# A decode block on one core: the last block of the modulation weight, split into uneven pieces on SyncE's and GpSimd's queues

## The chip, the cores and the metric

The kernel runs on one core of one Trainium2 chip. The metric is the device time in microseconds: 1050.39 us is the median of three runs of the kernel before (1050.29 to 1050.45).

## What is computed

One token passes through a transformer block with adaptive layer norms. The reference, cut to what matters (all in float32):

```python
mod = (_silu(c) @ w_mod).reshape(1, 6, 1, 640)      # sa, ca, ga, sb, cb, gb
h = _layernorm(x) * (1 + ca) + sa
x = x + ga * attention(h, k_cache, v_cache, wq, wo)  # 32 heads, 8192 positions, 192 wide
h = _layernorm(x) * (1 + cb) + sb
x = x + gb * (relu(h @ w1 + b1) ** 2 @ w2 + b2)      # 640 -> 1536 -> 640
```

`w_mod` is 640 x 3840. K and V cache are 32 x 8192 x 192 each, and they make nearly all of the 452 MB that the kernel reads.

## The kernel before, in words

**One stream of loads.** Every large input is laid out on the host as rows of 128 partitions and read once, in order, by transfers issued by SyncE's queue (`nc.sync.dma_start`, SP in the profile): `wm0` (L131), six pieces of `wm0x` (L134), then 53 chunks of the cache and of `wq` and `wo` (`load`, L236 to L253; the last chunk in two transfers), then `wm1`, `w1` and `w2` in several cuts each. They go into three slots of 16128 columns a partition, `slots` (L563), in turn: `wm0_t` in the first, chunk 0 in the second, chunk 1 in the third, chunk 2 again in the first. `load(n + 3)` is called after the work on chunk n (L436), so chunk 2 waits until the slot of `wm0_t` has been read for the last time, chunk 3 until chunk 0 has been worked off, and so on.

**The start.** `wm0` holds the first 1280 columns of `w_mod` (shift and scale of the first norm) as five blocks of 128 rows, the first block of `wq`, and small vectors. `mod(0, 2, wm0_t, wm0x_t)` (L193, called at L257) multiplies silu(c) with these columns on TensorE: four groups of 32 output partitions, each with its quarter of the 640 columns of both vectors, `DG` = 160 columns each. Blocks 0 to 3 are whole. Of the last block, `wm0` holds five of the eight quarters; the other three, `WX` = 480 columns, are held apart in `wm0x`: each of the block's 128 rows has one piece of 480 columns (1920 bytes). The table `XP` (L42) places the pieces: an entry (a, k, n) is one transfer of k rows to the partitions a, a+4, ..., with the first n of `SX` = 7 places a row. A place that no piece fills stays zero from the two memsets at L129 and L130, and the coefficients `cx` put silu(c) of the right row at each place and partition, so that 7 small matrix products with 64 partitions for each of two output groups (L211 to L214) add up what the block's missing quarters give. Then come the first norm, `query(0, ...)` (L273), which turns the first block of `wq` into the query of the first heads, and from there the loop over the chunks (L389).

**The loop.** For each chunk VectorE multiplies K with the query (`multiply`, L285) and sums over the 192 columns (`scores`, L293), GpSimd adds halves of 7/16 of the rows (L411), and TensorE applies V (`values`, L334) and `wo` (`attend`, L366 and L368).

**The end.** `w2` comes in six transfers, and in `finish` (L476) the matrix products of each wait for that transfer alone. After the last, two small operations of VectorE and the two transfers of the result follow.

**Partitions and DMA engines.** A transfer to 128 partitions is split over the core's 16 DMA engines in equal shares, 8 rows an engine. A transfer of fewer rows uses fewer engines: the trace has the eight rows of the first piece transfer on eight engines at once, those of three rows on three.

Of the kernel before, what the change touches and what calls it, by code (L numbers as in the profile page):

```python
# [13 lines left out]
P = 128  # L14
D = 640
# [4 lines left out]
G = 4  # L20
DG = D // G
FG = FF // G
KB = DG // 32
# [14 lines left out]
UNIT = E * DH  # L38
EXTRA = {"o": WO, "q": WQ}
SLOT = 84 * DH  # L40
SX = 7
XP = ((32, 8, 5), (0, 3, SX), (1, 3, SX), (2, 3, SX), (3, 3, 6), (33, 1, SX))  # L42
WX = 3 * DG
W0 = KB * 2 * D - WX
VPC = 5
LEAD_FROM = 1300
# [51 lines left out]


@with_exitstack  # L100
def block_kernel(ctx: ExitStack, tc: tile.TileContext, kept, kv, wm0, wm0x, wm1, w1, w2):
    nc = tc.nc
    const = ctx.enter_context(tc.tile_pool(name="const", bufs=1))
    work = ctx.enter_context(tc.tile_pool(name="work", bufs=2))
# [5 lines left out]
    def slot(name):  # L110
        taken.append(name)
        return kept["slots"][(len(taken) - 1) % 3]
# [12 lines left out]
    nc.gpsimd.memset(eps_t, EPS)  # L125

    wm0_t = slot("wm0_t")
    wm0x_t = wm0_t[:64, SLOT - SX * WX:]
    nc.vector.memset(wm0x_t[:, :SX // 2 * WX], 0.0)  # L129
    nc.gpsimd.memset(wm0x_t[:, SX // 2 * WX:], 0.0)  # L130
    nc.sync.dma_start(wm0_t[:, :wm0.shape[1]], wm0)  # L131
    r = 0
    for a, k, n in XP:
        nc.sync.dma_start(wm0x_t[a:a + 4 * k:4, :n * WX], wm0x[r:r + k, :n * WX])  # L134
        r += k

    small = const.tile([P, 2 * KB + SX + FB + KB], F32, name="small")
    nc.vector.tensor_copy(small, wm0_t[:, W0 + WQ:wm0.shape[1]])
    x_c, c_c, bbc = small[:, :KB], small[:, KB:2 * KB + SX], small[:, 2 * KB + SX:]

# [44 lines left out]
    e = const.tile([P, KB + SX], F32, name="silu")  # L185
# [7 lines left out]
    def mod(first, n, w, wx=None, between=lambda: None):  # L193

        ps = psum.tile([P, 512], F32, tag="q", name=f"ps_mod{first}", bufs=2)
        for b in range(KB):
            if b == 3:
                between()
            wb = w[:, b * n * D:(b + 1) * n * D]
            if wx is None or b < KB - 1:  # L200
                wb = wb.rearrange("p (m n) -> p m n", m=n)
                parts = [(g, slice(0, n * DG), wb[:, :, DG * g:DG * (g + 1)]) for g in range(G)]
            else:
                wb = wb[:, :n * 3 * DG].rearrange("p (m n) -> p m n", m=n)
                parts = [(g, slice(0, n * DG), wb[:, :, DG * g:DG * (g + 1)]) for g in range(2)] + [(2, slice(0, DG), wb[:, 0, 2 * DG:])]
            for g, at, wg in parts:
                nc.tensor.matmul(ps[32 * g:32 * (g + 1), at], e[:, b:b + 1].to_broadcast([P, 32]), wg,  # L207
                                 start=(b == 0), stop=(b == KB - 1 and (wx is None or g < 2)))
        if wx is not None:
            wx = wx.rearrange("p (s n) -> p s n", s=SX)  # L210
            for s in range(SX):  # L211
                for g, at, wg in ((2, slice(DG, 2 * DG), wx[:, s, :DG]), (3, slice(0, 2 * DG), wx[:, s, DG:])):
                    nc.tensor.matmul(ps[32 * g:32 * (g + 1), at], e[:64, KB + s:KB + s + 1].to_broadcast([64, 32]), wg,  # L213
                                     start=False, stop=(s == SX - 1))  # L214
        nc.vector.tensor_copy(mods[:, first:first + n], ps[:, :n * DG].rearrange("p (m n) -> p m n", m=n))

    def gate(m, w, steps):

        ps = psum.tile([P, 512], F32, tag="q", name="ps_gate", bufs=2)
        b = 0  # L220
        for n in steps:
            for b in range(b, b + n):
                for k in range(2):
                    nc.tensor.matmul(ps[64 * k:64 * (k + 1), :2 * DG], e[:, b:b + 1].to_broadcast([P, 64]),
                                     w[:, b, 2 * DG * k:2 * DG * (k + 1)], start=(b == 0), stop=(b == KB - 1))
            b += 1
            yield
        for g in range(G):
            r = slice(32 * g, 32 * (g + 1))
            nc.scalar.activation(m[r], ps[r, DG * (g % 2):DG * (g % 2 + 1)], AF.Copy)  # L230
        yield
# [23 lines left out]
    load(0)  # L255
    load(1)
    mod(0, 2, wm0_t, wm0x_t)  # L257
    ma = columns(mods[:, 0:2].rearrange("p m n -> p (m n)"), 2 * DG, "ma")
    h1 = layernorm(x_c, 1, lambda: ma[:, KB:, 0], lambda: ma[:, :KB, 0], "ln1")
# [129 lines left out]
    for n, (kp, nk, vp, nv, extra) in enumerate(PLAN):  # L389
# [3 lines left out]
        at = nk * DH + nv * UNIT  # L393
# [13 lines left out]
        if nk:  # L407
            multiply(kt, kp, nk)
            m = nk - POOL * nk // 16
# [34 lines left out]
    turn(NPAIR - 1)  # L444
    attend(*wo_t)
    mod(2, 3, wm1_t[:, KB * D:KB * 4 * D], between=gather)
    x1 = kept["x1"]
    nc.vector.tensor_mul(x1, att_t[0][:, :DG], mods[:, 2])
    nc.vector.tensor_add(x1, x1, x_t)

    last = gate(kept["gb"], gb_t, (2, 1, 2))
# [120 lines left out]
```

## Time and profile before

| | before |
|---|---|
| median of three runs | 1050.39 us |
| the profiled execution's own time | 1050.09 us |
| its span, first to last instruction | 1048.7 us |
| busy: VectorE, TensorE, GpSimd, ScalarE | 827.2, 491.7, 190.4, 44.9 us |
| HBM read | 451.82 MB |
| granted TensorE clock, mean | 0.72 |

A page of the profile gives busy times of each engine, the span in 40 slices, the DMA queues, the chain of work that ended last, and groups of instructions. "SPq" is the queue of SyncE that issues transfers; its duration is that of issuing, not of the transfer. q1 is the queue row on which SyncE's transfers run; q8 and q14 bring the engines' own instructions. In the view by windows, the share of DMA is that of the 16 engines together, and a packet counts where it starts, so that short windows with long packets read roughly.

### The profile page before, as it was taken

The numbers are of one execution on the slowest core, as the hardware profiler recorded it, in microseconds if no ns is written. First come the engines' busy times: TensorE is split into PE (matmuls) and PEld (weight loads), VectorE is DVE, ScalarE is ACT, GpSimd is POOL, SyncE is SP. The second block draws the span as 40 slices with busy tenths as digits, with TensorE's granted clock in tenths as the row PEclk, the third lists the DMA queues.
The fourth block names the chain that finished last, engine by engine and source line by source line (L and its number), as shares of the span: only waits on it lengthen the run. The fifth ranks groups of instructions, "written<-read, shape, count | busy, mean of one in ns | idle before, by whom it ended". The sixth has DMA issues, their size and how long they took to land.

```text
span 1048.7 us, 5220 instructions
## 1 busy us (share of the span) xinstructions
PE 491.7 (47%) x2162; PEld 136.0 (13%) x2162; DVE 827.2 (79%) x409; ACT 44.9 (4%) x122; POOL 190.4 (18%) x61
## 2 busy tenths in 40 slices
PE   3253334455352363436354366344445336436288
PEld 1010011111010010101011011011111002001023
DVE  1799878886959969888697895999887977988913
ACT  0100000000000000000000000000000000000001
POOL 1113121121212211212122121122221211311300
PEclk9676576777675686668766576676776767768689
DMA  9999999999999999999999999999999999999998
GB/s 408 431 434 433 432 433 433 440 437 439 436 437 431 431 433 432 433 433 429 435 439 436 436 432 432 434 431 433 433 434 431 436 448 434 433 433 431 423 425 365
DMA packets 9434, 452.16 MB, mean 431 GB/s; under 512 B 1066, under 2 KB 1326, under 8 KB 1710
## 3 DMA queue, kind: packets, MB, share of 16 engines
q1 hardware_dynamic: 9406, 451.83, 99.6%
q8 instruction: 17, 0.28, 0.1%
q14 instruction: 7, 0.05, 0.0%
q10 hardware_dynamic: 4, 0.00, 0.0%
HBM read 451.82 MB, written 0.00 MB: 431 GB/s over the span
## 4 chain that ended last, share of the span: by engine, by line
DMA 54%; DVE 33%; PE 12%; ACT 1%; issue 0%; SPq 0%; DVEq 0%; ACTq 0%
DMA slot<-in_kv 50%; DVE slot L285 17%; DVE sc L293 13%; PE ps_o L334 5%; DMA slot<-in_w 3%; PE ps_q L266 2%; PE att_a L366 2%; DMA slot<-in_wm 1%; DVE os L348 1%; PE ps_mx L309 1%; DVE om L346 1%; ACT p L317 0%; PE ps_mod L207 0%; PE att_a L368 0%; PE ps_mod L213 0%
## 5 line engine op out<-in xcount | busy, mean ns | idle before, releaser
L285 DVE TENSOR_TENSOR slot<-slot,qb 128x8064 f32<-128x8064 f32 (+19 forms) x81 | 419.7, 5212 | 127.0 <-DMA slot<-in_kv 121.8
L293 DVE TENSOR_REDUCE sc<-slot 128x25 f32<-128x4800 f32 (+21 forms) x109 | 333.9, 3096 | 0.4
L411 POOL TENSOR_TENSOR slot<-slot 128x1824 f32<-128x1824 f32 (+9 forms) x51 | 187.3, 3673 | 801.0 <-DVE slot L285 698.3
L334 PE MATMUL ps_o<-slot,p 128*32 128x512 f32 x1536 | 291.1, 724 | 70.4 <-DMA slot<-in_kv 60.8
L309 PE MATMUL ps_mx<-ident,mp 128*128 128x128 f32 x32 | 14.5, 452 | 346.4 <-DVE mp L307 346.4
L334 PEld LDWEIGHTS ps_o<-slot,p 128*32 128x32 f32 x1536 | 67.9, 130 | 268.7 <-issue 199.3
L366 PE MATMUL att_a<-slot,oW 128*32 128x512 f32 x96 | 66.5, 849 | 44.9 <-ACT oW L364 44.9
L266 PE MATMUL ps_q<-slot,ln_h 128*128 128x512 f32 x120 | 71.8, 758 | 27.2 <-DMA slot<-in_kv 25.0
L309 PEld LDWEIGHTS ps_mx<-ident,mp 128*128 128x128 f32 x32 | 5.6, 175 | 375.3 <-DVE mp L307 307.1
L317 ACT ACTIVATE p<-sc,nm 128x256 f32<-128x256 f32 x32 | 16.2, 507 | 650.3 <-DVE nm L311 650.3
L266 PEld LDWEIGHTS ps_q<-slot,ln_h 128*128 128x128 f32 x120 | 28.8, 250 | 67.4 <-issue 36.8
L346 DVE TENSOR_TENSOR om<-ps_o,mask 96x512 f32<-96x512 f32 x32 | 21.6, 675 | 8.9 <-PE ps_o L334 8.9
L311 DVE TENSOR_REDUCE nm<-ps_mx 128x1 f32<-128x128 f32 x32 | 9.3, 292 | 19.6 <-PE ps_mx L309 19.6
L366 PEld LDWEIGHTS att_a<-slot,oW 128*32 128x32 f32 x96 | 12.4, 144 | 82.3 <-ACT oW L364 47.6
L348 DVE TENSOR_REDUCE os<-om 96x64 f32<-96x512 f32 x32 | 21.8, 682 | 1.1
L356 DVE TENSOR_REDUCE oT<-ps_oT 128x3 f32<-128x96 f32 x16 | 4.0, 248 | 18.6 <-PE ps_oT L352 18.6
L322 PE MATMUL ps_sum<-ident,wide 128*128 128x128 f32 x16 | 7.5, 466 | 22.4 <-ACT wide L320 22.4
L352 PE MATMUL ps_oT<-ident,os 96*128 96x96 f32 x16 | 5.0, 314 | 25.3 <-DVE os L348 25.2
L207 PE MATMUL ps_mod<-slot,silu 128*32 128x480 f32 (+2 forms) x78 | 9.2, 612 | 14.3 <-DVE silu L189 14.3
L368 PE MATMUL att_a<-slot,oW 128*96 128x384 f32 x32 | 14.2, 525 | 0.0
L364 ACT ACTIVATE oW<-oT,r 128x96 f32<-128x96 f32 x16 | 5.9, 371 | 172.8 <-DVE oT L356 172.8
L267 ACT ACTIVATE qb<-ps_q 128x512 f32<-128x512 f32 x12 | 7.2, 597 | 131.9 <-PE ps_q L266 131.9
(84 smaller groups left out, 92.0 us busy)
## 6 DMA issues: line engine op xcount, KB each, us to landing
slot<-in_kv SPq DMA_DIRECT2D x38, 8064.0 KB, 35.3
slot<-in_kv SPq DMA_DIRECT2D x11, 8000.0 KB, 37.4
slot<-in_kv SPq DMA_DIRECT2D x2, 7872.0 KB
slot<-in_kv SPq DMA_DIRECT2D x1, 6144.0 KB, 22.7
slot<-in_wm SPq DMA_DIRECT2D x1, 4480.0 KB
slot<-in_wm SPq DMA_DIRECT2D x1, 4257.0 KB, 12.4
slot<-in_kv SPq DMA_DIRECT2D x1, 3264.0 KB
slot<-in_kv SPq DMA_DIRECT2D x1, 3072.0 KB
```

The lines of the kernel that those rows point to most:

```text
L266: nc.tensor.matmul(ps, h1[:, b:b + 1].to_broadcast([P, P]), w[:, b], start=(b == 0), stop=(b == KB - 1))
L285: nc.vector.tensor_mul(pr, pr, q[:, None, :].to_broadcast([P, b - a, DH]))
L293: nc.vector.tensor_reduce(sc[:, a % SRING:a % SRING + b - a], src[:, a - first:b - first], axis=AX.X, op=ALU.add)
L309: nc.tensor.transpose(ps[:, :P], mp.to_broadcast([P, P]), ident)
L311: nc.vector.tensor_reduce(nm, ps[:, :P], axis=AX.X, op=ALU.max, negate=True)
L317: nc.scalar.activation(p, s[:, :, None].to_broadcast([P, NPOS, 32 // E]), AF.Exp, bias=nm, accum_out=sp[:, h % 2:h % 2 + 1])
L334: nc.tensor.matmul(ps_t[h][32 * g:32 * (g + 1)], p[:, E * j:E * (j + 1)].rearrange("p e r -> p (e r)"), t[:, g], start=(j == 0), stop=last)
L346: nc.vector.tensor_mul(om[:n], ps_t.pop(h)[:n].rearrange("p (d e) -> p d e", e=E), mask[:n, None, :].to_broadcast([n, ED, E]))
L348: nc.vector.tensor_reduce(os_[:n, h % 2], om[:n], axis=AX.X, op=ALU.add)
L366: nc.tensor.matmul(att_a[96:, :512], oW[:, j], w[:, j, :512], start=(first and j == 0), stop=(last and j == NV - 1))
L368: nc.tensor.matmul(att_a[:96, :NV * (D - 512)], oW.rearrange("p j r -> p (j r)"), w[:, :, 512:], start=first, stop=last)
L411: nc.gpsimd.tensor_add(half, half, kt[:, m:, DH // 2:])
```

## The change

640 columns of the last block are taken out of `wm0` in place of 480: the third and fourth quarter of both vectors. `wm0` loses 160 columns of every partition. The 128 pieces are now 640 columns (2560 bytes) each, the places a row are `SX` = 12, and they may lie on all 128 partitions in place of 64.

57 pieces come in three transfers of SyncE: five rows with 3 places, three rows with 12, three rows with 2. The other 71 (and one place of zeros) come in three transfers of GpSimd's queue, two rows with 12 places each, to the partitions 28 and 64, 2 and 92, 29 and 65 (the table `XG`: rows of the transfer ahead, first partition, step). Ahead of each of these goes a tiny transfer of 7, 6 and 6 rows with two runs of 16 numbers a row, to columns that nobody reads. The rows of the new input `wm0y` are padded by 16 numbers after each place, which are not loaded, so a row of 12 places is 12 runs of 2560 bytes.

TensorE does two products of 320 columns over 128 partitions for each of the 12 places, and one product of 160 columns less in the last block. The two memsets cover 128 partitions and 12 x 640 columns in place of 64 and 7 x 480.

```diff
-SX = 7
-XP = ((32, 8, 5), (0, 3, SX), (1, 3, SX), (2, 3, SX), (3, 3, 6), (33, 1, SX))
-WX = 3 * DG
+SX = 12
+XP = ((32, 5, 3), (0, 3, SX), (1, 3, 2))
+XG = ((7, 28, 36), (6, 2, 90), (6, 29, 36))
+WX = 4 * DG
...
-    wm0x_t = wm0_t[:64, SLOT - SX * WX:]
+    wm0x_t = wm0_t[:, SLOT - SX * WX:]
     nc.vector.memset(wm0x_t[:, :SX // 2 * WX], 0.0)
     nc.gpsimd.memset(wm0x_t[:, SX // 2 * WX:], 0.0)
     nc.sync.dma_start(wm0_t[:, :wm0.shape[1]], wm0)
...
     for a, k, n in XP:
         nc.sync.dma_start(wm0x_t[a:a + 4 * k:4, :n * WX], wm0x[r:r + k, :n * WX])
         r += k
+    for i, (k, a, step) in enumerate(XG):
+        rest = wm0_t[32 * i:32 * i + k, wm0.shape[1]:wm0.shape[1] + 64].rearrange("p (a n) -> p a n", a=2)
+        nc.gpsimd.dma_start(rest[:, :, :16], wm0x[:k, :64].rearrange("p (a n) -> p a n", a=2)[:, :, :16])
+        to = wm0x_t[a:a + step + 1:step].rearrange("p (s n) -> p s n", n=WX)
+        nc.gpsimd.dma_start(to, wm0y[i, :, :, :WX])
...
-                wb = wb[:, :n * 3 * DG].rearrange("p (m n) -> p m n", m=n)
-                parts = [(g, slice(0, n * DG), wb[:, :, DG * g:DG * (g + 1)]) for g in range(2)] + [(2, slice(0, DG), wb[:, 0, 2 * DG:])]
+                wb = wb[:, :n * 2 * DG].rearrange("p (m n) -> p m n", m=n)
+                parts = [(g, slice(0, n * DG), wb[:, :, DG * g:DG * (g + 1)]) for g in range(2)]
...
             for s in range(SX):
-                for g, at, wg in ((2, slice(DG, 2 * DG), wx[:, s, :DG]), (3, slice(0, 2 * DG), wx[:, s, DG:])):
-                    nc.tensor.matmul(ps[32 * g:32 * (g + 1), at], e[:64, KB + s:KB + s + 1].to_broadcast([64, 32]), wg,
+                for g in (2, 3):
+                    wg = wx[:, s, 2 * DG * (g - 2):2 * DG * (g - 1)]
+                    nc.tensor.matmul(ps[32 * g:32 * (g + 1), :n * DG], e[:, KB + s:KB + s + 1].to_broadcast([P, 32]), wg,
                                      start=False, stop=(s == SX - 1))
...
+        "wm0y": np.pad(np.stack([xw[a:a + step + 1:step] for _, a, step in XG]), ((0, 0), (0, 0), (0, 0), (0, 16))),
```

More of the change, by code (lines that the diff above doesn't have):

```diff
@@ L100, in block_kernel @@
 @with_exitstack
-def block_kernel(ctx: ExitStack, tc: tile.TileContext, kept, kv, wm0, wm0x, wm1, w1, w2):
+def block_kernel(ctx: ExitStack, tc: tile.TileContext, kept, kv, wm0, wm0x, wm0y, wm1, w1, w2):
     nc = tc.nc
@@ L540 @@
     cc = column(c, KB)
-    at = [(s, a + 4 * i) for a, k, n in XP for s in range(n) for i in range(k)][:P]
+    at = [(s, a + 4 * i) for a, k, n in XP for s in range(n) for i in range(k)]
+    at = (at + [(s, a + i * step) for _, a, step in XG for s in range(SX) for i in range(2)])[:P]
     xs, xp = np.array(at).T
@@ L544 @@
     xw, cx = np.zeros((P, SX, WX), np.float32), np.zeros((P, SX), np.float32)
-    xw[xp, xs] = np.concatenate([last[:, 1, 2 * DG:3 * DG], last[:, 0, 3 * DG:], last[:, 1, 3 * DG:]], axis=1)
+    xw[xp, xs] = last.reshape(P, 2, G, DG)[:, :, 2:].transpose(0, 2, 1, 3).reshape(P, WX)
     cx[xp, xs] = cc[:, KB - 1]
@@ L549 @@
         "kv": np.concatenate(kv),
-        "wm0": np.concatenate([m0[:, :(KB - 1) * 2 * D], last[:, 0, :3 * DG], last[:, 1, :2 * DG],
+        "wm0": np.concatenate([m0[:, :(KB - 1) * 2 * D], last[:, 0, :2 * DG], last[:, 1, :2 * DG],
                                wq[0], column(A_x, KB), cc, cx, column(B_b1, FB), column(B_b2, KB)], axis=1),
         "wm0x": np.concatenate([xw[a:a + 4 * k:4] for a, k, _ in XP]).reshape(-1, SX * WX),
+        "wm0y": np.pad(np.stack([xw[a:a + step + 1:step] for _, a, step in XG]), ((0, 0), (0, 0), (0, 0), (0, 16))),
         "wm1": np.concatenate([rows(wm[:, 5 * D:], KB), rows(wm[:, 2 * D:5 * D], KB)], axis=1),
```

## The prediction

> **What bounds the kernel now.** I read the page's slices and queues first, then the end of the chain of waits, then the DMA share by windows around the end, then the start by timeline.
>
> ```profile
> DMA  9999999999999999999999999999999999999998
> q1 hardware_dynamic: 9406, 451.83, 99.6%
> q8 instruction: 17, 0.28, 0.1%
> HBM read 451.82 MB, written 0.00 MB: 431 GB/s over the span
> 1016.93 28.71 DMA slot<-in_w
> 1045.68 0.66 PE p_long L490 x16
> 1046.36 0.29 DVE slot L502
> ```
>
> All 16 DMA engines are busy in every slice: one stream of transfers is the kernel. 431 GB/s are 26.9 GB/s an engine. The chain ends with the last cuts of `w2` and 2.6 us of work behind them (1048.7 less about 1046.1), so whatever moves the last landing moves the end by as much. And the last landing is that of the slowest DMA engine, not of the mean:
>
> ```profile
> 1042.00:1043.00 1.00, 0.92 (x28) 0.95 (x32) 0.00 (x0) 0.00 (x0) 0.00 (x0) 1.00 1.00 406
> 1043.00:1043.50 0.50, 0.50 (x24) 0.50 (x20) 0.00 (x0) 0.00 (x0) 0.00 (x0) 1.00 0.92 367
> 1043.50:1044.00 0.50, 0.50 (x23) 0.50 (x17) 0.00 (x0) 0.00 (x0) 0.00 (x0) 1.00 0.81 325
> 1044.00:1045.00 1.00, 0.96 (x32) 0.50 (x21) 0.45 (x2) 0.00 (x0) 0.00 (x0) 1.00 0.77 315
> 1045.00:1045.50 0.50, 0.12 (x7) 0.00 (x0) 0.20 (x1) 0.00 (x0) 0.00 (x0) 1.00 0.74 284
> 1045.50:1045.80 0.30, 0.12 (x4) 0.12 (x8) 0.00 (x0) 0.00 (x0) 0.00 (x0) 1.00 0.75 258
> 1045.80:1046.00 0.20, 0.20 (x12) 0.20 (x13) 0.00 (x0) 0.00 (x0) 0.00 (x0) 1.00 0.36 109
> 1046.00:1046.20 0.20, 0.20 (x12) 0.04 (x4) 0.00 (x0) 0.00 (x0) 0.00 (x0) 1.00 0.08 22
> ```
>
> The last column but one is the DMA share. From 1043 to 1044 it falls to about 0.77 and stays there: four engines of 16 are through almost 3 us before the other twelve. Idle share times length adds up to 0.04 + 0.10 + 0.23 + 0.13 + 0.08 + 0.13 + 0.18 = 0.9 us. That is all that any better split over the engines can bring, since the bytes stay; 0.2% of the time, about what a measurement of this kernel can tell from no change, are 2.1 us.
>
> Why four are early is in the packet records, which the views only sum up. Each row starts 3 to 4 ns after the one before it on its engine, so the 16 chains can be followed. How far each is behind the earliest (1043.14) when its last row has landed, and why:
>
> ```
> 2.81 2.61 2.84                            engines 0-2: pieces of wm0x (39, 32, 32); the last two one 8 KB fetch each
> 2.99 2.95 | 2.69 | 0.79 | 0.01            engines 3-7: 5 pieces each; two 16 KB fetches | three of 8 KB | one | none
> 2.60 2.65 2.75 2.74 2.79 2.79 0.25 0.00   engines 8-15: no pieces; six with two 16 KB fetches each, two with none
> ```
>
> Which engine within a line is which the records don't tell. A fetch of instructions stops one engine's rows:
>
> ```profile
> q8 instruction: 1, 0.02, 4.8%
> q14 instruction: 1, 0.01, 1.0%
> ```
>
> These are windows of 1.2 us (from 62.4) and 2 us (from 119) with one fetch each: 4.8% of 16 engines over 1.2 us are 0.92 us, and 1.0% over 2 us 0.32. In the records the row behind it is late by another 0.3 to 0.5 us, 1.4 us in all for 16 KB. Sixteen such fetches before the end go round eight engines twice. The engines 0 to 2 have none, and so carry the pieces.
>
> **The change part by part.**
>
> ```profile
> slot<-in_kv SPq DMA_DIRECT2D x1, 8000.0 KB, 35.9
> slot<-in_kv SPq DMA_DIRECT2D x1, 6144.0 KB, 22.7
> slot<-in_wm SPq DMA_DIRECT2D x1, 4257.0 KB, 12.4
> slot<-in_kv SPq DMA_DIRECT2D x38, 8064.0 KB, 35.3
> 0.73 0.40 SPq L131 DMA_DIRECT2D slot<-in_wm  x1
> 1.42 1.69 POOL L130 MEMSET slot<- 64x1920 f32 x1
> 1.93 1.26 DVE L129 MEMSET slot<- 64x1440 f32 x1 [0.24 <-issue]
> 3.28 4.12 SPq L134 DMA_DIRECT2D slot<-in_wm0x  x6
> 7.45 27.21 SPq L249 DMA_DIRECT2D slot<-in_kv  x3
> 13.18 0.18 DVE L138 COPY small<-slot 128x34 f32<-128x34 f32 x1 [9.99 <-DMA slot<-in_wm]
> 14.34 4.76 PE L207 MATMUL ps_mod<-slot,silu 128*32 128x320 f32 x38 [14.34 <-DVE silu L189]
> 19.02 3.96 PE L213 MATMUL ps_mod<-slot,silu 64*32 64x160 f32 x28
> 34.34 0.33 SPq L249 DMA_DIRECT2D slot<-in_kv  x1
> 34.98 12.96 DVE L285 TENSOR_TENSOR slot<-slot,qb 128x12288 f32<-128x12288 f32 x1 [5.14 <-ACT qb L267]
> 47.97 10.21 DVE L293 TENSOR_REDUCE sc<-slot 128x36 f32<-128x6912 f32 x2
> 58.21 0.33 SPq L249 DMA_DIRECT2D slot<-in_kv  x1
> ```
>
> *Bytes.* Every engine gives up 8 x 160 x 4 = 5120 bytes of `wm0`, 0.19 us at 26.9 GB/s. A piece of 2560 bytes is 0.095 us. By SyncE, five rows on engines 0 to 4 and three rows on 0 to 2, as the rows of before fell: 17 pieces on 0, 1 and 2, and 3 on 3 and 4; engines 5 to 7 lose their 5 x 1920 bytes, 0.36 us. GpSimd's 72 places (one of them zeros) are two rows a transfer; no row of the trace shows which engines take them. I take it that each row goes to one engine, and that the two pairs of neighbours (partitions 28 and 64, 29 and 65) are one pair of early engines, with 24 pieces each, and 2 and 92 engine 0 and another early one, with 12 each; the other case is rival C. The Trainium skill, "DMA: Bandwidth & Descriptors", The descriptor swizzle, gives these partitions to engines 7 and 8 and to 0 and 15; no run here shows it. Then, behind the earliest of before: 0 has 29 x 0.095 = 2.76, less 0.19, 2.57; the two with 24 have 2.28 + 0.25 - 0.19 = 2.3; the engines with two fetches and no pieces have at most 2.79 - 0.19 = 2.60 (two of 3 to 7 drop from 2.99 to 2.99 - 0.36 - 0.19 = 2.44, if they are two of 5 to 7). The slowest goes from 2.99 to 2.60: 0.4 us gained. If a twice-fetched engine is 3 or 4, it keeps 2.99 - 0.19 - 0.07 = 2.73: 0.26.
>
> *Memsets and issues.* At 1.26 us for 1440 and 1.69 for 1920 columns, 3840 take 3.4 us on each engine: done at 5.3 and 4.8 in place of 3.2 and 3.1. SyncE's pieces wait for both; three issues of 4.12 / 6 = 0.69 us end at 7.4, as before, so the first chunk is issued at the same time, 5 us before `wm0` has landed. Cost nothing, with that cover. GpSimd's six issues have no row; the nearest are SyncE's, 0.33 to 0.69 us each, and GpSimd's own operations, 0.1 to 1.7. I take 1 us each: issued from 4.8 to about 11. Behind them on GpSimd is only the memset of `att_s`, needed past 1026.
>
> *The start's chain.* TensorE waits for all pieces before L213, and behind it stand the norm, the query, SyncE's chunk 2 (34.34) and VectorE's first multiply (34.98). L213 was 7 places x 2 passes in 3.96 us, 0.28 a pass, the two groups side by side; 12 x 2 passes are 6.8: +2.8 us. `wm0` lands later on the engines where GpSimd's pieces get between its rows: 12 to 24 x 0.095 = 1.1 to 2.3 us, less 0.19. In all the query is 3.7 to 4.9 us late. Who waits: chunk 3 is issued when VectorE is through with chunk 0, at 58.21, now at 62 to 63. The stream needs it when chunk 2 is in: 4257 KB, 240 of pieces (128 x 1920 bytes), 6144, 8000 and 8064 are 27.35 MB, 63.5 us at 431 GB/s, from the first packet at 1.7: 65.2. `wm0` landed 12.4 us after its issue and its bytes need 10.1, so an issue is worth at most 2.3 us ahead. 62 + 2.3 is 64.3: covered, with 0.9 us left; at the upper end, 65.4, a gap of 0.2. Later chunks have more: VectorE has caught up by 106.
>
> *Notices and turns.* What a DMA of another queue costs an engine amid SyncE's rows no row shows for data. Between SyncE's own transfers the notice is a record of 4 bytes, 9 ns; after a fetch, 0.3 to 0.5 us are lost. With 24 pieces on an engine in a few turns: 0 to 0.5 us a turn. I take 0.05 to 0.1, nearest to the rows that also go from HBM to the slots, and keep 1.5 us for the range.
>
> *Rule against trace.* Fetches come in between two rows of one SyncE transfer (62.51, in chunk 2), so a turn of q1 is one row, 1.3 to 2.4 us. The Trainium skill, "DMA: Bandwidth & Descriptors", has under Queues, rings and completion order that an engine drains a whole packet of typically 9 to 17 descriptors before it turns to another queue; by that 12 pieces and their notice pass in one turn, and the sum above stands. The same page of the Trainium skill, under SWDGE vs HWDGE vs iDMA, keeps a packet of GpSimd's path at 4096 bytes or less, and by that each piece of 2560 takes a turn of its own: the first rival.
>
> *Sum.* 1050.09 (the profiled execution's own time; the median of the runs is 0.3 above) - 0.4 + 0.1 to 0.3 = 1049.8 to 1050.0, on the median's scale 1050.2. Its own range: 1049.7 to 1052.0.
>
> **The rivals.** *A: pieces that take turns with rows (slower).* If an engine takes one piece, then one row of SyncE's, 24 pieces and 6 notices need 30 turns. From 6.5 us on, the two engines with 24 have about 4 rows of `wm0` left, then 8 of chunk 0 (48 KB, 1.8 us each) and 8 of chunk 1 (62.5 KB, 2.4 us): 20 turns, until q1 is empty at 1.7 + 19.09 MB / 431 GB/s = 46; then the rest goes at once. L213 starts at 48.5 in place of 19.02, chunk 2 is issued 32 us late, at 66.6, and the stream stands for about 22 us; chunk 3, at 90.5, is again some 4 us late: 1077. With two pieces a turn it is 15 turns, L213 at 33, gaps of 6.5 and 4.6 us: 1061. It decides from 5 us of delay of L213's start on. For it: the row-wise turns and the 12 separate runs a row. Against: nothing in this trace has two streams of data at once. Chance 0.25.
>
> *B: every engine pays for the notices.* The same page of the Trainium skill, under Why a DMA increments its semaphore by 16 and not by 1, has GpSimd's transfers post a notice on all 16 engines, however few carry data. Six turns at the 0.5 us lost after a fetch are 3 us on every engine, in place of the 0.1 to 0.3 of the sum: 1053.0. Against: the 9 ns of notices in the trace. Chance 0.08.
>
> *C: it doesn't do what it says.* If a pair of GpSimd's rows falls on engines with two fetches, or all on 0 and 1, one engine ends at 2.75 + 24 x 0.095 = 5.0, or 53 x 0.095 = 5.0, in place of 2.99, less 0.19: 1050.4 + 1.9 = 1052.3. Chance 0.06.
>
> **How the numbers follow.** Forecast 0.60, A 0.25, B 0.08, C 0.06, faster by over 2.1 us 0.01, since 0.9 us is all that a balance can give. Same: 0.60, 0.05 of C and 0.01 of B: 0.66. Slower: 0.25, 0.07 and 0.01: 0.33. The range goes from 1049.7 to 1062, which takes in B, C and A with two pieces a turn; half of A, 0.13, is left out.
>
> **What would show it.** Right: L213 starts within 2 us of 19 and takes 6.5 to 7 us; chunk 2 issued at 38 to 39.5, chunk 3 at 62 to 63; no window from 40 to 90 with a lower DMA share; the share near the end falls later than 1043 and faster. Wrong: TensorE waiting at L213 for `in_wm0y` (A); engines later than 1046 from the first 20 us on, all alike (B) or two alone (C).

## The result, and the profile after

The changed kernel takes 1081.19 us (median of 5 runs, 1080.34 to 1082.61), the kernel before beside it 1050.29 us (1050.15 to 1050.45): a ratio of 1.0296, interval 1.0281 to 1.0312, so about 31 us slower. The forecast of 1050.2 and its range up to 1062 are both missed. Rival A, with 1077, is what happened.

The page of the changed kernel, its slices and queues:

```profile
DMA  9738999999999999999999999999999999999998
GB/s 400 307 153 344 451 425 426 449 424 443 428 425 449 420 444 430 428 442 428 434 436 432 442 423 440 437 430 438 430 431 446 426 432 435 432 435 438 426 424 352
...
q1 hardware_dynamic: 9386, 451.65, 96.8%
...
q0 software_dynamic: 432, 0.19, 0.1%
...
L220 PE MATMUL ps_mod<-slot,silu 128*32 128x320 f32 x48 | 9.5, 569 | 30.6 <-DMA slot<-in_wm0y 30.6
```

A slice is 27 us. From the fifth on the row of DMA is as before; all of the loss lies in the second to the fourth. 0.19 MB of GpSimd's queue (q0) hold up a stream of 452 MB: the products of the pieces (L220; L213 in the kernel before) stood 30.6 us for `in_wm0y`. The chain of waits of the changed kernel says what lies between (start, length, what):

```profile
4.72 9.84 issue
14.58 0.70 POOL slot L139
...
16.41 32.78 DMA slot<-in_wm0y
49.20 0.55 issue
49.75 9.48 PE ps_mod L220 x48
...
63.77 7.22 PE ps_q L273 x10
71.01 0.61 ACT qb L274
```

A transfer of 60 KB has taken 32.8 us. The timeline of the changed kernel, with the rows that answer to those of before:

```profile
1.43 3.30 POOL L131 MEMSET slot<- 128x3840 f32 x1
...
2.44 3.26 DVE L130 MEMSET slot<- 128x3840 f32 x1 [0.75 <-issue]
...
5.73 2.29 SPq L135 DMA_DIRECT2D slot<-in_wm0x  x3
...
14.66 4.48 PE L213 MATMUL ps_mod<-slot,silu 128*32 128x320 f32 x36 [14.66 <-DVE silu L195]
...
17.55 0.60 POOL L141 DMA_DIRECT2D slot<-in_wm0y  x1
...
49.75 9.47 PE L220 MATMUL ps_mod<-slot,silu 128*32 128x320 f32 x48 [30.61 <-DMA slot<-in_wm0y]
...
71.01 36.42 SPq L256 DMA_DIRECT2D slot<-in_kv  x3
...
71.64 12.96 DVE L292 TENSOR_TENSOR slot<-slot,qb 128x12288 f32<-128x12288 f32 x1 [5.79 <-ACT qb L274]
```

The start is as it was: block products (L213 here, L207 before) from 14.66. GpSimd issues its six transfers from 14.58 to 18.15. The pieces' products begin at 49.75 in place of 19.02, chunk 2 is issued at 71.01 in place of 34.34, and chunk 3 at 94.87 in place of 58.21. What that does to the stream is in the windows of the changed kernel (window, length, busy PE, PEld, DVE, ACT, POOL, granted clock, DMA share, GB/s):

```profile
40.00:45.00 5.00, 0.00 (x0) 0.00 (x0) 0.00 (x0) 0.00 (x0) 0.00 (x0) 0.50 0.99 427
45.00:50.00 5.00, 0.25 (x2) 0.21 (x4) 0.00 (x0) 0.00 (x0) 0.00 (x0) 0.50 0.19 72
50.00:55.00 5.00, 5.00 (x20) 1.89 (x18) 0.00 (x0) 0.00 (x0) 0.00 (x0) 0.50 0.00 0
55.00:60.00 5.00, 4.21 (x30) 1.73 (x26) 0.71 (x2) 0.00 (x0) 0.00 (x0) 0.95 0.00 0
60.00:65.00 5.00, 1.99 (x6) 1.31 (x7) 2.44 (x11) 1.54 (x2) 0.00 (x0) 0.73 0.01 3
65.00:70.00 5.00, 5.00 (x8) 1.94 (x8) 0.82 (x2) 0.00 (x0) 0.00 (x0) 0.59 0.00 0
70.00:75.00 5.00, 0.97 (x3) 0.15 (x1) 3.36 (x1) 1.88 (x2) 0.00 (x0) 1.00 0.70 245
...
90.00:95.00 5.00, 0.00 (x0) 0.00 (x0) 4.97 (x3) 0.00 (x0) 0.56 (x1) 0.50 0.00 0
```

Idle share times length: 4.05 + 5 + 5 + 4.95 + 5 + 1.5 + 5 = 30.5 us, roughly, since a packet counts where it starts; summed over the packet records the stream stands 29.2 us between 40 and 100. The kernel is 30.9 us slower. It stands twice: 25 us from about 46 on, until chunk 2 is asked for, and 4 us before chunk 3. These are the two gaps of rival A. The clock column shows one thing that no rival had: TensorE is granted 0.50 while it waits, and keeps that for the first 5.7 of the 9.5 us of L220 (a mean of 0.95 over 55 to 60 leaves half a us at 0.50).

**Why 60 KB took 33 us.** The DMA view of the changed kernel, from 15 to 45 and from 45 to 50:

```profile
q1 hardware_dynamic: 239, 12.80, 98.6%
q0 software_dynamic: 209, 0.08, 1.0%
...
q1 hardware_dynamic: 20, 0.26, 12.0%
q0 software_dynamic: 223, 0.10, 7.2%
```

In 30 us, 239 packets of SyncE's queue and 209 of GpSimd's: nearly one for one. When q1 runs dry, the other 223 go in 4 us. The packet records show the same engine by engine. One of them reads, from 18.08 on: a row of 49152 bytes (1.8 us), a q0 record of 8 bytes at 19.90, a row, 4 bytes at 21.72, a row, 5120 bytes (196 ns) at 23.53, a row, 5120 bytes at 25.54, and so on to its last row at 44.85. The 4-byte notice that ends one of SyncE's transfers takes a turn like a row. **A turn is one record, whatever its size.** And there are 432 = 16 x 27 records: 36 with two pieces each (5120 bytes), 19 of 128 bytes (the rows of the tiny transfers), 96 notices of 4 bytes (six on each engine), and 281 of 8 bytes, which fill up the engines without data. So every engine has 27 turns to take, not only the two with 24 pieces. By the time that its last row of chunk 1 was through, each had taken only 13 or 14 of them; the rest, the third transfer of pieces among them, followed when SyncE's queue was empty.

### The profile page after: what moved, and what is told of

It reads as the page before. It is cut to its first block, busy times and chain, and to the rows that moved or that the text cites. A ratio compares the mean times of both kernels' runs of the same rounds, so it can differ in the third digit from the quotient of the medians.

```text
span 1080.9 us, 5272 instructions
## 1 busy us (share of the span) xinstructions
PE 498.3 (46%) x2180; PEld 138.0 (13%) x2180; DVE 828.8 (77%) x409; ACT 44.9 (4%) x122; POOL 195.8 (18%) x67
## 4 chain that ended last, share of the span: by engine, by line
DMA 53%; DVE 35%; PE 9%; issue 1%; ACT 1%; POOL 1%; DVEq 0%; SPq 0%; POOLq 0%; ACTq 0%
DMA slot<-in_kv 47%; DVE slot L292 18%; DVE sc L300 14%; PE ps_o L341 5%; DMA slot<-in_wm0y 3%; DMA slot<-in_w 3%; PE ps_q L273 1%; PE ps_mod L220 1%; PE att_a L373 1%; DVE os L355 1%; PE ps_mx L316 1%; ACT p L324 1%; DVE om L353 1%; DVE nm L318 0%; PE ps_sum L329 0%
## 5 line engine op out<-in xcount | busy, mean ns | idle before, releaser
L373 PE MATMUL att_a<-slot,oW 128*32 128x512 f32 x96 | 63.8, 819 | 44.9 <-ACT oW L371 44.9
L222 DVE COPY mods<-ps_mod 128x320 f32<-128x320 f32 (+1 forms) x2 | 1.1, 575 | 48.4 <-PE ps_mod L220 44.6
L220 PE MATMUL ps_mod<-slot,silu 128*32 128x320 f32 x48 | 9.5, 569 | 30.6 <-DMA slot<-in_wm0y 30.6
L213 PE MATMUL ps_mod<-slot,silu 128*32 128x480 f32 (+1 forms) x76 | 8.9, 603 | 14.7 <-DVE silu L195 14.7
L375 PE MATMUL att_a<-slot,oW 128*96 128x384 f32 x32 | 14.4, 532 | 0.0
```

Source lines behind the costliest of these rows:

```text
L220: nc.tensor.matmul(ps[32 * g:32 * (g + 1), :n * DG], e[:, KB + s:KB + s + 1].to_broadcast([P, 32]), wg, start=False, stop=(s == SX - 1))
L373: nc.tensor.matmul(att_a[96:, :512], oW[:, j], w[:, j, :512], start=(first and j == 0), stop=(last and j == NV - 1))
L375: nc.tensor.matmul(att_a[:96, :NV * (D - 512)], oW.rearrange("p j r -> p (j r)"), w[:, :, 512:], start=first, stop=last)
```

## The experiments

Theory from here on: the time is that of 27 turns against SyncE's rows (cut short where SyncE's queue runs dry first), and everything else in the change costs nothing. Rivals: the late issue (GpSimd stood 9.85 us before its first transfer); turns by bytes, not by records; a price for each record on its engine (rival B); the added work of TensorE and the memsets. The four columns in the middle of this table are times of the trace; the first row is the kernel before.

| kernel | q0 records an engine | last record | products start, take | chunk 2 issued | chunk 3 issued | time, us |
|---|---|---|---|---|---|---|
| before | 0 | | 19.0, 4.0 | 34.3 | 58.2 | 1050.3 |
| after | 27 | 48.8 | 49.8, 9.5 | 71.0 | 94.9 | 1081.2 |
| e1, SyncE only | 0 | | 18.9, 7.2 | 36.7 | 60.6 | 1050.8 |
| e2, issued early | 27 | 48.8 | 49.4, 9.2 | 70.2 | 94.0 | 1080.8 |
| e3, rows cut in four | 27 | 32.9 | 33.5, 8.3 | 52.7 | 76.5 | 1064.8 |
| e6, two runs a row | 15 | 33.7 | 34.3, 9.5 | 55.6 | 79.5 | 1066.6 |
| e9, e6 without tiny | 9 | 26.6 | 27.3, 8.2 | 46.4 | 70.2 | 1058.2 |
| e12, e6, chunk 0 in two | 15 | 23.7 | 24.3, 8.9 | 44.6 | 68.5 | 1055.9 |
| e10, e9, chunk 0 in two | 9 | 21.4 | 22.1, 6.8 | 41.0 | 64.8 | 1053.3 |
| e8, early, rows cut in eight | 27 | 19.9 | 20.5, 6.7 | 39.3 | 63.2 | 1051.6 |
| e7, e6, rows cut in four | 15 | 19.5 | 20.0, 6.7 | 38.5 | 62.4 | 1051.1 |

**e1: all pieces by SyncE.** The 640 columns, the products and the memsets of the change, without GpSimd's transfers.

```diff
-XP = ((32, 5, 3), (0, 3, SX), (1, 3, 2))
-XG = ((7, 28, 36), (6, 2, 90), (6, 29, 36))
+XP = ((32, 8, 4), (0, 3, SX), (1, 3, SX), (2, 3, 8))
...
-    for i, (k, a, step) in enumerate(XG):
...
```

> All 128 pieces of 640 columns come by SyncE (eight rows with 4 places, three with 12, three with 12, three with 8); GpSimd's six transfers are gone. Turns (GpSimd's records wait for a row of SyncE's each): with them gone L213 starts at 19 to 20 us and takes 6.5 to 6.8, chunk 2 is issued at 37 to 38, chunk 3 at 61 to 62, no gap in the stream; engines 0 to 2 carry 36 x 0.095 = 3.4 us of pieces, less 0.2, so 1050.4 to 1051.5. Rival, extra work (the 10 more passes of TensorE and the longer memsets make the delay): slower than 1055.

1050.8 us (1050.65 to 1050.88), ratio 1.0005, interval 0.9996 to 1.0015. Its timeline, the products (but for the first two) and the later chunks:

```profile
19.48 6.64 PE L214 MATMUL ps_mod<-slot,silu 128*32 128x320 f32 x46
36.75 71.07 SPq L250 DMA_DIRECT2D slot<-in_kv  x5
```

The bytes, the memsets and 24 products of 128 rows are not the loss. The 31 us belong to GpSimd's transfers.

**e2: the same transfers, issued earlier.** In the changed kernel the first tiny transfer, whose columns lie in the same slot, was issued only after the last of SyncE's pieces had landed (14.17 by the packet records; issue at 14.58). Here the tiny ones write a tile of their own, and GpSimd issues from 4.67 to 9.3.

```diff
+    spare = const.tile([P, 64], F32, name="spare")
...
-        rest = wm0_t[32 * i:32 * i + k, wm0.shape[1]:wm0.shape[1] + 64].rearrange("p (a n) -> p a n", a=2)
+        rest = spare[32 * i:32 * i + k].rearrange("p (a n) -> p a n", a=2)
```

> The tiny transfers write a tile of their own, so GpSimd's six transfers no longer wait for SyncE's pieces: issued from about 5 us in place of 14.6. Turns: 27 records an engine, from 9.6 us on 2 rows of wm0, 8 of chunk 0 and 8 of chunk 1 are 18 turns, the other 9 records still wait until SyncE's queue is empty at 46; L213 starts at 47 to 50, 1078 to 1082. Rival, late issue (the pieces are late since GpSimd issued them 9 us late): L213 at 41, about 1072.

1080.78 us (1080.1 to 1081.45). The products in its timeline:

```profile
49.39 9.16 PE L221 MATMUL ps_mod<-slot,silu 128*32 128x320 f32 x48 [28.98 <-issue]
```

The issue is ten us earlier and the time 0.4 us shorter, which two runs that lie 1.35 us apart can't tell from nothing. The late issue falls. The first q0 record comes at 9.1, and 103 are through by 15, but the rest wait for chunk 0 and chunk 1 all the same.

**e3: SyncE's rows a quarter as long.** The transfers of GpSimd as in the changed kernel; chunks 0 and 1 are loaded in four column parts each.

```diff
-            cuts = (m,) if n + 1 < len(PLAN) else ((PLAN[n][3] + 1) // 2 * UNIT, m)
+            cuts = tuple(m * i // 4 // 4 * 4 for i in range(1, 4)) + (m,) if n in (0, 1) else (m,) if n + 1 < len(PLAN) else ((PLAN[n][3] + 1) // 2 * UNIT, m)
```

> The loads of chunk 0 and chunk 1 are cut into four column parts each, so that their rows are 12 and 16 KB (0.45 and 0.6 us) in place of 48 and 62.5; GpSimd's transfers as in the changed kernel, issued at 14.6. Turns: 27 records need 20 rows until 27 us and 7 of 0.6: L213 at 32 to 35, chunk 2 issued at about 55, a gap of 8 to 10 us and 4 to 5 more at chunk 3: 1062 to 1066. Rivals, late issue or a slow rate of GpSimd's small records: L213 at 49 to 50, 1081.

1064.76 us (1064.58 to 1064.93). Its timeline:

```profile
33.52 8.31 PE L220 MATMUL ps_mod<-slot,silu 128*32 128x320 f32 x48 [13.41 <-issue]
52.67 36.43 SPq L256 DMA_DIRECT2D slot<-in_kv  x3
```

Nothing of GpSimd's has changed, only what its records alternate with. The 27 turns now take 14.4 us (18.5 to 32.9) in place of 30.3.

**e4: the single-packet option.** The option on all six transfers of GpSimd.

```diff
-        nc.gpsimd.dma_start(to, wm0y[i, :, :, :WX])
+        nc.gpsimd.dma_start(to, wm0y[i, :, :, :WX], single_packet=True)
...
```

> GpSimd's six transfers are sent as one packet each (an option of the transfer); all else as in the changed kernel, issued at 14.6. Turns: six turns an engine in place of 27, 4 or 5 in chunk 0's rows and the rest in chunk 1's: L213 at 28 to 32, 1058 to 1063; if the notice is a turn of its own, 12 turns, L213 at 43 to 46, 1074 to 1078. Rivals, late issue or a slow rate: L213 at 49 to 50, 1081.

1081.43 us, records of the same number and sizes, products at 49.74. Neither expectation came true: the option changes nothing in the records here, so it does not test the turns. It is a miss that says only how not to make fewer records.

**e5: the price of a record.** The kernel before, and twelve tiny transfers of GpSimd for which nobody waits.

```diff
+    spare = const.tile([P, 64], F32, name="spare")
+    for i in range(12):
+        rest = spare[8 * i:8 * i + 7].rearrange("p (a n) -> p a n", a=2)
+        nc.gpsimd.dma_start(rest[:, :, :16], wm0x[:7, :64].rearrange("p (a n) -> p a n", a=2)[:, :, :16])
```

> The kernel before with twelve tiny transfers of GpSimd added and nothing else (no data pieces, nobody waits for them; the output is the reference's). Theory (records of GpSimd's queue cost an engine next to nothing; what was lost in the changed kernel is only the wait for the pieces): about 24 records an engine, nearly as many as the 27 of the changed kernel, go between SyncE's rows, L213 of the kernel before stays at 19, and the time is within 0.3 us of before, 1050.0 to 1050.6. Rival B (every notice or turn stops its engine for 0.3 to 0.5 us): twelve notices or more on each engine, 3.6 to 6 us, 1054 to 1056.

1050.43 us (1050.37 to 1051.05), ratio 1.0002, interval 0.9993 to 1.0012. Its DMA view from 15 to 45:

```profile
q1 hardware_dynamic: 244, 12.96, 99.7%
q0 software_dynamic: 222, 0.01, 0.5%
```

The same alternation, 384 records in all (24 an engine), the last one at 48.8, and no time lost: 12.96 MB in 30 us are 432 GB/s. Only the products start later than expected, at 19.87 in place of 19.02, and chunk 3 is issued at 59.23 in place of 58.21, which the stream doesn't notice. Twelve notices on each engine at rival B's price would have been 6 us. A record is cheap to an engine; it is only slow to arrive.

**e6: fewer records.** Each row of GpSimd comes as two runs of 3840 columns (15360 bytes) in place of twelve of 640; the tiny transfers as in e2.

```diff
-        to = wm0x_t[a:a + step + 1:step].rearrange("p (s n) -> p s n", n=WX)
-        nc.gpsimd.dma_start(to, wm0y[i, :, :, :WX])
+        to = wm0x_t[a:a + step + 1:step].rearrange("p (s n) -> p s n", n=SX // 2 * WX)
+        nc.gpsimd.dma_start(to, wm0y[i, :, :, :SX // 2 * WX])
...
```

> The changed kernel with GpSimd's rows as two runs of 3840 columns in place of twelve of 640, and the tiny transfers writing a tile of their own, so that they are issued from about 5 us. Theory (a turn of an engine is one record, whatever its bytes, against one row of SyncE): if a run travels as one record, 15 records an engine in place of 27; in the early experiment 244 records of all engines, 15 each, were through by 25 us, so the last piece lands at 25 to 30, the piece products start there, chunk 2 is issued 19 to 21 us later, at 45 to 50, and the time is 1051 to 1058. Rival (bytes set the turn, 4 to 5 KB each): the runs are cut into as many turns as before, the piece products start near 49 and the time stays at 1080.

1066.63 us (1065.45 to 1067.57). Its page and timeline:

```profile
q0 software_dynamic: 240, 0.19, 0.1%
34.30 9.51 PE L221 MATMUL ps_mod<-slot,silu 128*32 128x320 f32 x48 [13.81 <-issue]
```

The same 0.19 MB in 15 records an engine: a run of 15360 bytes is one record, 573 ns long, and passes in one turn. Against e2, with the same bytes and the same issue, the products start 15 us earlier. That falsifies turns by bytes. The landing was expected at 25 to 30 and the time at 1051 to 1058; it came at 33.7, since 15 turns need all eight rows of chunk 0 and some of chunk 1 on the slowest engine. The expectation rests on a misreading of e2: of its records 184 had started by 25 us, and 244 only by 30.

**e7 and e8: the turns made short enough.** e7 is e6 with chunks 0 and 1 in four parts; e8 is e2 (27 records) with both chunks in eight (e3's line with 8 for 4):

```diff
+            cuts = tuple(m * i // 8 // 4 * 4 for i in range(1, 8)) + (m,) if n in (0, 1) else (m,) if n + 1 < len(PLAN) else ((PLAN[n][3] + 1) // 2 * UNIT, m)
```

> As the two-run experiment, and chunks 0 and 1 loaded in four column parts each, so that SyncE's rows are a quarter as long. Theory: 15 records an engine against rows of 0.4 to 1.3 us land by 17 to 21, the piece products start at 19 to 22, no gap in the stream, and the time is that of the kernel without GpSimd's transfers or up to 0.4 us better by the balance: 1049.8 to 1050.8. If bytes set the turn: as with short rows alone but issued 9 us earlier, piece products at 24 to 26, 1052 to 1056. If something other than the late pieces costs the time, it stays above 1060.

> The pieces as in the changed kernel (twelve runs a row, 27 records an engine), tiny transfers into a tile of their own, and chunks 0 and 1 loaded in eight column parts each. Theory (one record a row): the row of chunk 0 is 6 KB, 0.24 us, so that the 27 records land 8 to 10 us after the first at 9.1, by 17 to 21; the piece products start by 22 and the time is 1050.0 to 1051.5, the more so as the stream has no gap. Rival (the count of records, or their bytes, limits GpSimd's queue by itself): the landing stays near 33, as with four parts, and the time near 1064.

e7: 1051.12 us (1050.86 to 1051.43), ratio 1.0008, interval 0.9999 to 1.0017. e8: 1051.61 us (1051.11 to 1051.98), ratio 1.0012, interval 1.0004 to 1.0021. The timeline of e7, then of e8:

```profile
20.29 6.38 PE L221 MATMUL ps_mod<-slot,silu 128*32 128x320 f32 x46
38.48 71.07 SPq L257 DMA_DIRECT2D slot<-in_kv  x5
```

```profile
20.49 6.74 PE L221 MATMUL ps_mod<-slot,silu 128*32 128x320 f32 x48
```

With all 27 records and all six transfers in place, but against rows of 6 to 8 KB, 30 of the 31 us are gone. No other cause is needed. Both are a little above what was expected, by 0.3 us (e7) and 0.1 (e8); e11 says why for four parts, and no run has the kernel before with eight.

**e11: the price of short rows.** The kernel before with e3's line and nothing else.

```diff
+            cuts = tuple(m * i // 4 // 4 * 4 for i in range(1, 4)) + (m,) if n in (0, 1) else (m,) if n + 1 < len(PLAN) else ((PLAN[n][3] + 1) // 2 * UNIT, m)
```

> The kernel before with chunks 0 and 1 loaded in four column parts each and nothing else. If the 0.8 us by which the two-run experiment with short rows stays above the kernel before is the price of the shorter rows (48 more rows and six more notices on each engine), this kernel is 0.5 to 0.9 us above before: 1050.8 to 1051.2. If the price is that of GpSimd's records instead, it stays at 1050.2 to 1050.4.

1051.17 us (1050.81 to 1051.55), ratio 1.0009, interval 1.0000 to 1.0018: as much as e7. 48 more rows and six more notices an engine cost about 0.9 us, at the edge of what the interval can tell from nothing. e7 less e11, each beside runs of the kernel before with a median of 1050.27, is what the change is worth when its pieces arrive in time: 0.05 us, which is nothing. The ends of the two streams still differ; the window from 1044 to 1045 of e7, then of e11:

```profile
1044.00:1045.00 1.00, 1.00 (x40) 1.00 (x34) 0.00 (x0) 0.00 (x0) 0.00 (x0) 1.00 0.95 383
```

```profile
1044.00:1045.00 1.00, 1.00 (x38) 0.91 (x28) 0.00 (x0) 0.00 (x0) 0.00 (x0) 1.00 0.84 338
```

In e7 the engines end closer together. By the packet records the last row lands 0.75 us behind the mean of the engines in e7 and 0.96 in e11, so the better balance is there and gains 0.2 us, too little to be measured in the time.

**e9 and e10: without the tiny transfers.** e9 is e6 without them (the first line below); e10 is e9 with chunk 0 in two halves (both lines).

```diff
-        nc.gpsimd.dma_start(rest[:, :, :16], wm0x[:k, :64].rearrange("p (a n) -> p a n", a=2)[:, :, :16])
...
+            cuts = (m // 2 // 4 * 4, m) if n in (0,) else (m,) if n + 1 < len(PLAN) else ((PLAN[n][3] + 1) // 2 * UNIT, m)
```

> The two-run experiment (rows of two runs of 3840 columns, chunks loaded whole) without the three tiny transfers, so nine records an engine in place of fifteen; the three transfers can be issued when the memsets are done, near 6 us. Theory (one record a turn): in the two-run experiment 15 records an engine landed by 33.7; three pass with the rows of wm0 (1.24 us each), six more take turns with chunk 0's rows of 1.8 us: landing at 23 to 26, the piece products start there, chunk 2 is issued 19 to 21 us later at 43 to 46, about when the stream runs out, and chunk 3 about 4 us too late: 1052 to 1058. Rival (the bytes of the pieces, not the number of records, set the landing): landing stays near 33 and the time near 1066.

> As the one without tiny transfers, and chunk 0 loaded as two halves (rows of 24 KB, 0.9 us). Theory: six records against rows of 0.9 us land by 18 to 20.5, the piece products start by 21, nothing in the stream stands still and the time is 1049.9 to 1050.8. What is left to see is the 0.4 us of balance: only eight more rows an engine than in the changed kernel, so if the extra rows of the four-part and eight-part experiments were what kept them at 1051.1 and 1051.6, this one is at least 0.3 us below the four-part one.

e9: 1058.17 us (1057.3 to 1058.89). e10: 1053.32 us (1053.01 to 1053.43). With 9 records an engine the products start at 27.3 and 22.1. e9 ends just beyond what was expected (products at 23 to 26, up to 1058). e10 is a miss, by 2.5 us over 1050.8. Nothing in its stream stands still, and chunk 3 is in time. Its windows from 12 to 20 show another loss:

```profile
12.00:16.00 4.00, 0.00 (x0) 0.00 (x0) 0.51 (x3) 0.22 (x1) 0.00 (x0) 1.00 0.90 281
16.00:20.00 4.00, 3.62 (x28) 1.38 (x32) 0.29 (x2) 0.00 (x0) 0.00 (x0) 1.00 1.01 366
```

The engines are busy, at 281 and 366 GB/s. In the records a row of 24576 bytes takes up to 1.6 us there (0.91 is usual), a run of pieces up to 1.13 us (0.57), and this on all 16 engines. By 46 us e10 has moved 17.90 MB and e1 18.74: 0.84 MB, 1.9 us at 434 GB/s. The rest is balance: at the end the last row of e10 lands 1.8 us behind the mean of the engines (0.75 in e7). When chunk 1 has landed, three engines are 2.9 us behind the earliest, four 1.7 to 2.1, and the other nine less than 1, as if six engines had a row of pieces each, three of them beside the 17 pieces that they have from SyncE. The Trainium skill, "DMA: Bandwidth & Descriptors", Why a DMA increments its semaphore by 16 and not by 1, has GpSimd's transfers of few rows go to consecutive engines, on from a cursor that goes round; the trace of the changed kernel agrees: the first tiny transfer has its seven rows on seven engines, among them the five with SyncE's pieces, and the two rows of pieces behind it lie on two others. By that the tiny transfers of 7, 6 and 6 rows move the rows of pieces off the engines that SyncE has filled, all but one row: in e6 only one of the six shares an engine with 17 pieces of SyncE's.

**e12: the tiny transfers again.** e10 with its three tiny transfers, so only they differ.

```diff
+    spare = const.tile([P, 64], F32, name="spare")
...
+        rest = spare[32 * i:32 * i + k].rearrange("p (a n) -> p a n", a=2)
+        nc.gpsimd.dma_start(rest[:, :, :16], wm0x[:k, :64].rearrange("p (a n) -> p a n", a=2)[:, :, :16])
```

> As the half-row experiment without tiny transfers, but with the three tiny transfers again (into a tile of their own): the two kernels differ in nothing else. In that experiment and in the other one without tiny transfers, rows of all sixteen engines took up to 1.7 times as long from 11 to 25 us, which cost 2 us; in the two-run experiments with tiny transfers no row was slow. If the tiny transfers (by the engines or moments that they give to the pieces) keep that away: no slow rows, 15 records against rows of 0.9 us land by 22 to 24.5, the piece products start by 25, and the time is 1050.3 to 1051.5. If the halves of chunk 0 or the moment of issue made the slow rows: 1052.5 to 1054 again.

1055.88 us (1055.01 to 1056.96). Its windows, and the products in its timeline:

```profile
12.00:16.00 4.00, 0.41 (x4) 0.20 (x8) 0.80 (x4) 0.22 (x1) 0.00 (x0) 1.00 0.97 412
16.00:20.00 4.00, 3.92 (x36) 1.31 (x28) 0.00 (x0) 0.00 (x0) 0.00 (x0) 1.00 0.99 422
...
64.00:68.00 4.00, 0.00 (x0) 0.00 (x0) 4.00 (x2) 0.00 (x0) 0.19 (x1) 0.50 0.60 258
68.00:72.00 4.00, 3.13 (x5) 1.61 (x6) 3.34 (x4) 0.60 (x2) 0.00 (x0) 0.50 0.77 258
```

```profile
24.29 8.86 PE L221 MATMUL ps_mod<-slot,silu 128*32 128x320 f32 x48 [4.37 <-issue]
```

The slow rows are gone (412 and 422 GB/s), so they do hang on the absence of the tiny transfers; why is open. The time is a miss nevertheless, at 1055.9 in place of 1050.3 to 1051.5. The landing (23.7) and the start of the products (24.3) came as expected, but TensorE had stood, its clock was low, and the products took 8.86 us. Chunk 2 is issued at 44.6 and chunk 3 at 68.5, and the stream stands for 0.6 and 2.2 us by the records. Another part, 1.5 us as a mean over the engines, went to 30 slow rows at the start of chunk 2, which started as chunk 1 ran out, and of chunk 3 (2.7 to 4.1 us for rows that usually take 2.4). Some 1.3 of the 5.6 us are not accounted for. So the cover of the start's chain (how late it may be before the stream has nothing to load) ends before a start of the products at 24.3; at 22.1 (e10) it still held, though there the stream was itself 1.9 us late.

## Why the prediction was wrong

- *What bounds the kernel* held: the stream, and what asks for its next chunk.
- *Memsets and issues* held, at 3.30 and 3.26 us on the two engines (3.4 forecast) and 0.55 to 0.70 us for an issue of GpSimd (1 us taken). What it missed is that the first tiny transfer, into slot 0, waits for SyncE's pieces until 14.58. By e2 that is worth no more than 0.4 us here.
- *The start's chain* held for its own work: in e1 the products take 7.2 us from 18.94 (6.8 forecast), chunk 3 is issued at 60.6, and the time is 0.5 us above before. The cover of chunk 3 was put at about 5 us. e8 (chunk 3 issued 5.0 us later than before, no idle stream) and e12 (10.3 us later, 2.8 us of it) bracket it. What the step lacked is that a late start also makes the products slower: 9.47 us at a clock of 0.50 and then 1.00, against 6.7 us in e7 and e8, nearly all of it at 1.00. The Trainium skill, "TensorE: Matmul & The Clock Gate", Part 1, says that the gate falls to half after some 3.4 us without work and opens after as long under load. The trace agrees on the two levels, 0.50 in the wait and 1.00 again under load, but less on the times: the clock fell 2.2 us after the last block product (19.14 to 21.34) and came back 5.7 us after the start of L220, in the other runs that waited 3.2 (e9) to 5.8 us (e6) after.
- *Notices and turns* is the step that failed. It priced "a few turns" at 0.05 to 0.1 us each, as a cost to the engine. That price was right, even high (e5: 24 records an engine for 0.2 us, within the interval of nothing). But the turn was not the cost; the wait for it was. It asked what GpSimd's records do to SyncE's rows and not what SyncE's rows do to GpSimd's records, on which TensorE waits: the last record landed 30.3 us after the first, and the products started at 49.75 in place of 19.02.
- *Rule against trace.* The row was read rightly: a fetch comes in between two rows, so a turn of q1 is one row. The other side of the turn was taken from the Trainium skill, "DMA: Bandwidth & Descriptors", Queues, rings and completion order, whose packet of 9 to 17 descriptors would have let twelve pieces pass at once. The trace disagrees: two pieces (5120 bytes) a turn, or one notice of 4 bytes, or one filler of 8. Under SWDGE vs HWDGE vs iDMA the same page of the Trainium skill has packets of preferably at most 4096 bytes; that is no limit to a turn here, since e6 passes 15360 bytes in one. The measurement decides: it is one record, and what a record holds must be read from the packets.
- *Rival A* named the mechanism, the place and the sequence: products at 48.5 (49.75 measured), chunk 2 at 66.6 (71.0), chunk 3 at 90.5 (94.9), 1077 (1081.2). Its count was off in a way that did not show. It gave 30 turns to the two engines with 24 pieces; in fact two pieces share a record, and the fillers and notices give all 16 engines 27. It also began the turns at 6.5 us, where the first record came at 18.5. Since either number needs more rows than chunks 0 and 1 have, the queue's running dry from 46 on set the landing in both, and that the count didn't matter is luck. The 4 us that it lacked are 1.2 us of landing and notice, and 3.2 us from there to chunk 2 (21.3 in place of 18.1), most of it the slower products. The chance of 0.25 was too small: its only counter-argument, that the trace shows no two streams of data at once, is no argument on either side.
- *Rival B* was right that every engine gets a notice from each transfer (96 = 6 x 16, as the Trainium skill, "DMA: Bandwidth & Descriptors", Why a DMA increments its semaphore by 16 and not by 1, has it), and wrong in their price (e5).
- *Rival C* did not happen: the pieces lie as the prediction took it. The packet records of the changed kernel, followed engine by engine, have the first and the third transfer's pieces on the same two engines, 24 pieces on each and none of SyncE's, and the second's 12 and 12 on one engine with 17 pieces of SyncE's and one with none. The Trainium skill, "DMA: Bandwidth & Descriptors", The descriptor swizzle, which the prediction names beside this, describes one transfer to 128 partitions and not one of two rows.
- *The balance*, forecast at 0.4 us, shows as 0.2 us in the records of e7 against e11. In the changed kernel itself it is moot, since all engines have run empty before chunk 2 starts at 72, and they start again together.

No version tried beats the kernel before: the nearest, e1, e7 and e11, are 0.5 to 0.9 us above it.

## What to carry to other kernels

A small transfer on a second queue did not cost the time of its bytes: here it cost the number of its records on an engine times the length of one row of the queue that it shares the engines with, up to the moment when that queue runs dry, and the fillers on engines without data count. Before such a transfer is put ahead of a due time, count its records and multiply; then lower either factor, with longer runs (fewer records) or shorter rows of the large transfers around it (e3, e6, e7), but the latter has a price of its own (e11). Where TensorE waits for it, look also at what the wait does to its clock.

## What was not expected of the hardware

- A transfer of GpSimd's queue with two rows of data put records on all 16 engines: 9 an engine for three transfers of two 15360-byte runs a row, 27 for three of twelve 2560-byte runs and three tiny ones; 281 of 432 records were 8 bytes long.
- From GpSimd's first issue to the first record of its queue passed 3.9 us in the changed kernel (14.58 to 18.51), 4.4 in e2 and 4.1 in e9.
- Without the tiny transfers, rows on all 16 engines ran at 281 GB/s together for some us while GpSimd's pieces landed (e10), with them at 412 (e12). This was not settled: the tiny transfers give the pieces other engines and other moments, and no run here tells the two apart.
